# One fused kernel on one core: the order of the first batch's plan, with w3 times w_out moved to its front

## The chip, the core and the metric

The kernel runs on one core of one Trainium2 chip. The core has TensorE (PE, matrix products into PSUM banks), VectorE (DVE), ScalarE (ACT), GpSimd (POOL) and SyncE (SP). ACT, POOL and above all SP issue DMA transfers, which 16 DMA engines carry out. Each engine executes its instructions in order and waits on semaphores for the others. The metric is the device time of one execution in microseconds; lower is better.

## The reference

```python
scores  = scale * x @ state^T;  a  = softmax(scores)      # 8 batches, 8 heads, 512 tokens, 32 state rows, D = 64
xread   = a @ state
scores2 = scale * state @ x^T;  a2 = softmax(scores2)
sread   = a2 @ x
x       = concat([xread, sread], rows), heads side by side   # 4608 x 512
# first FFN: w1, w2 512 x 1024, w3 1024 x 1024, w_out 1024 x 512
a = x @ w1;  b = x @ w2;  h = (a * b) @ w3;  x = h @ w_out
# second FFN: w_gate, w_val 512 x 1536, w_out2 1536 x 512
out = (sigmoid(x @ w_gate) * (x @ w_val)) @ w_out2
```

The weights come as 64-bit floats and are turned into 32-bit ones on the chip. x and state are float32.

## The kernel before

The work is rearranged so that much of it is done once. Since nothing nonlinear stands between w3 and w_out, their product **wp** (1024 x 512) is made once, and y = u wp with u = a * b. The attention's read of the state, times w1 or w2, is the softmax weights times a small product of state and w1 or w2 per batch: a **set** (`StateWeights`, tiles sw), four sets of 256 columns for a batch. The a and b products of a batch are therefore softmax weights (aT) times sets.

Nearly all large products run in split form: each operand is kept as a high and a low part (hi by a ScalarE copy that rounds, lo by a VectorE subtraction), and hi hi + hi lo + lo hi is summed in PSUM, three matmuls in place of one (`products`). A plain float32 product of the same size shows up as two matmul instructions, each of which takes longer.

**The stages.** `plan_start` does the first batch's attention and its a, b and u, and makes wp. Then `ffn1` runs for each batch t: with `slots`, a table of small pieces of other work hung in front of its steps 0 to 11. Steps 0 to 7 (JF = 8) are the a and b products with u = a * b, and steps 8 to 11 (KM = 4) the y products. For t = 0 the steps 0 to 7 are left out, as `plan_start` did them; its y products carry, in their slots, the next batch's sets and attention: at step 8 the end of the plan (`after_wp`), the turned state read (`sreadt`), sets 0 and 1 and the fetches for sets 2 and 3; x turned ahead of steps 8 and 9, scores and the first part of the softmax and sets 2 and 3 at step 10, the rest of the softmax and the split of aT at step 11. Behind all batches follows the second FFN in a stage of its own.

**The plan.** `plan_start` doesn't issue instructions in program order. It lists steps with an engine, an estimated cost and dependences (`plan.add`), and `Plan.order` works out an order from them: PE's and SP's steps keep the order of the list, those of ACT, DVE and POOL are taken greedily, the one with the longest path behind it first. The instructions are then issued in that order by hand. The list before:

1. x and state of batch 0 are loaded, 18 filler transposes on PE (`keep_clock`), x is turned (`xt`), state is turned, scores, both softmaxes (`scores`, `soft1` to `soft3`, `scores2`, `scores3`), 50 fillers.
2. Quarters of w1 and w2 (`quarter(q)`: four loads of 0.52 MB each, converted by `convert` to float32, stored for later batches to w12_d), then `make(q)`, the set, kept in plain float32 (tag swp); 24 fillers ahead of the first products; `pab(j)`: the a and b products for two j per set, plain, with ACT copying a to asb and DVE multiplying it by b to uw. The exponentials of the second softmax are turned (`a2t`) and the state read (`sread`) in between.
3. w_out in eight tiles (`wo_load`, `wo_split`: high part wo, low part wol), w3 in sixteen half rows (`w3_load`, and `w3_turn`: four transposes on PE, then high and low part w3t). `wp_sum(f, ks)` adds 24 matmuls for four k into one PSUM bank, for each of the eight rows f of wp in two halves; `wp_out` writes wp's high and low parts.
4. The u of all j are split into high and low parts (`u_split`), next batch's x is loaded (`load_x`, eight transfers), and quarters 0 and 1 of w1 and w2 are fetched back from w12_d for batch 1 (`nxt.fetch`).

A conversion is two ACT passes (lines 196 and 197) and three DVE passes (198, 202, 206). Raw 64-bit tiles have seven homes (`raw_tile`: three in pool cv, two in pw, two in the buffers that later hold aT); `Ring` tells a step which earlier step must free its buffer. Turned w3 tiles have three buffers and the set's and w3's PSUM tiles two banks.

Of the kernel before, what the change touches and what calls it, by code (L numbers as in the profile page):

```python
# [17 lines left out]
DRAM = bass.MemoryType.DRAM  # L18

# [98 lines left out]
def tile_state_attention__then__gated_ffns(  # L118
# [144 lines left out]
    with tc.manual_schedule(engines={mybir.EngineType.PE}):  # L263
# [15 lines left out]
        def attention(b, plain=False):  # L279
# [4 lines left out]
            def xt(g):  # L284
                def turn():
                    if g == 0:
# [186 lines left out]
            return before, after  # L473
# [16 lines left out]
        def state_turn(h4):  # L490
            pt = z["p", h4] = ps_main.tile([P, 512], F32, tag="m", name="pt")
# [72 lines left out]
        u0 = []  # L564

        def plan_start(cur, nxt):
# [4 lines left out]
            raws, rs, ms, wqs = Ring(7), Ring(2), Ring(3), Ring(2)  # L571
            ats, mains, ys_, asbs, w3s = Ring(2), Ring(4), Ring(2), Ring(2), Ring(3)
            cell = {}

# [5 lines left out]
            def raw_tile(n):  # L580
                if n % 7 < 3:
                    return cv.tile([P, 512, 2], U32, name="raw", bufs=3)
                if n % 7 < 5:
                    return pw.tile([P, 512, 2], U32, name="raw", bufs=2)
                return at.tile([P, 512, 2], U32, tag=f"aT{n % 7 - 5}", name="raw")

            def convert(src, place, *deps):
                n = len(raws.users)
                raw_free, raw_users = raws.take()
# [3 lines left out]
                def load():  # L593
                    c["raw"] = raw_tile(n)
# [8 lines left out]
                got = add("sp", 0.48, load, raw_free, load=LOAD)  # L603
# [12 lines left out]
            def load_half(i):  # L616
# [8 lines left out]
            xs = [add("sp", 0.48, lambda i=i: load_half(i), load=1.7) for i in range(2)]  # L625

            zs = [
                add("sp" if j < 2 else "act", 0.45, lambda j=j: load_z(0, j, (nc.sync, nc.scalar)[j // 2]), load=0.4)
                for j in range(4)
            ]  # L630

# [5 lines left out]
            placed = []  # L637
            for g in range(G):
                placed.append(add("act", 0.52, lambda g=g: place_x(g), xs[g // 2], *placed[-1:]))

            wq_users = []

            def quarter(q):
                free, users = wqs.take()
                wq_users.append(users)
# [8 lines left out]
                for i in range(4):  # L654
                    a, h = divmod(i, 2)
                    src = (w1, w2)[a][2 * h * P : 2 * (h + 1) * P, 2 * q * WQ : 2 * (q + 1) * WQ]
                    d, _ = convert(src.rearrange("(k p) f -> p k f", p=P), lambda i=i: place(i), free, *out[:1])
# [12 lines left out]
            def keep_clock(n):  # L670
                def go():
                    if "clock" not in cell:
                        cell["clock"] = ps_main.tile([P, 512], F32, tag="m", name="clock")
# [5 lines left out]
            clock_free, clock_users = mains.take()  # L679
            keep_clock(18)  # L680
            turned = []
            for g in range(G):
                free, users = ats.take()
                parts = xt(g)
                p = chain(parts[:1], free, placed[g])
                turned.append(chain(parts[1:], p))
                users.append(turned[-1])
            free, users = mains.take()
            p = add("pe", 0.44, lambda: state_turn(0), zs, free)
            st_out = add("act", 0.49, lambda: state_out(0), p)  # L690
            users.append(st_out)
            free = [ats.take() for _ in range(2)]
            parts = scores()
            p = chain(parts[:1], [f for f, _ in free], turned, st_out)
            d = chain(parts[1:], p)
            soft = chain(soft1() + soft2() + soft3(), d)
            e2 = [chain(scores2(k), p) for k in range(2)]
            for k in range(2):
                free[k][1].extend([d, e2[k]])
            r2 = chain(scores3(), e2)  # L700
            keep_clock(50)

            quarters = [quarter(0)]
            sets = {}

            def make(q):
# [5 lines left out]

                def out(k):
                    if k == 0:
                        cur.done[q] = [pb.tile([P, 2, 2, WQ], F32, tag="sw0", name="swp", bufs=4)]
                    copy("act", cur.done[q][0][:, k].rearrange("p a f -> p (a f)"), cell["ps", q][k])

                p = add("pe", 1.0, product, [f for f, _ in free], quarters[q], st_out)
                wq_users[q].append(p)
                o = []  # L720
                for k in range(2):
                    o.append(add("act", 0.49, lambda k=k: out(k), p, *o))
                    free[k][1].append(o[-1])
                sets[q] = o

            uw = {}

            def pab(j):
                ps = []
                for a in range(2):  # L730
# [7 lines left out]
                    ps.append((add("pe", 1.76, product, free, sets[j // 2], soft), users))  # L738
# [6 lines left out]
                def mult():  # L745
                    asb = cell["asb", j]
                    cell["uw", j] = (
                        pu.tile([P, 512], F32, tag="u", name="uw", bufs=2 * JF) if j < JF - 1 else asb
                    )
                    nc.vector.tensor_tensor(  # L750
                        out=cell["uw", j], in0=asb, in1=cell["pab", j, 1], op=ALU.mult
                    )
# [5 lines left out]
                users.append(o1)  # L758
                uw[j] = o1
# [19 lines left out]
            zs1 = []  # L779
            make(0)  # L780
            keep_clock(24)
            quarters.append(quarter(1))
            pab(0)
            pab(1)
            make(1)
            for k in range(2):
                free, users = ats.take()
                parts = a2t(k)
                p = chain(parts[:1], free, e2[k], soft, *([cell["a2", 0]] if k else []))
                cell["a2", k] = chain(parts[1:], p)  # L790
                users.append(cell["a2", k])
            quarters.append(quarter(2))
            pab(2)
            pab(3)
            make(2)
            free, users = ats.take()
            parts = sread()
            p = chain(parts[:1], free, cell["a2", 0], cell["a2", 1])
            users.append(chain(parts[1:], p, r2))
            quarters.append(quarter(3))  # L800
            zs1 = [
                add("sp", 0.45, lambda j=j: load_z(1, j, nc.sync), st_out, load=0.4) for j in range(4)
            ]
            pab(4)
            pab(5)
            make(3)
            free, users = mains.take()
            p = add("pe", 0.44, lambda: state_turn(1), zs1, free)
            users.append(add("act", 0.49, lambda: state_out(1), p))
            for k in range(HALF):  # L810
                wo_load(k)
            w3_load(0)
            pab(6)
            pab(7)

            wo = {}

            def wo_tile(k, i):
                if "wo" not in cell:
                    cell["wo"] = pw.tile([P, JF, DM], F32R, name="wo0", bufs=1)  # L820
                    cell["wol"] = [
                        pb.tile([P, 2, DM], F32R, tag="sw1", name="wol", bufs=4) for _ in range(JF // 2)
                    ]
                return cell["wol"][k // 2][:, k % 2] if i else cell["wo"][:, k]
# [43 lines left out]
            def wp_sum(f, ks):  # L868
                start = ks[0] == 0
                if start:  # L870
                    wp_users[f] = mains.take()
                js = sorted({2 * f + k // 4 for k in ks})

                def product():
                    if start:
                        cell["wp", f] = ps_main.tile([P, 512], F32, tag="m", name="pwp")
                    pairs = [
                        (
                            [t[:, k % 4] for t in cell["w3t", 2 * f + k // 4]],
                            (wo_tile(k, 0), wo_tile(k, 1)),  # L880
                        )
                        for k in ks
                    ]
                    products((cell["wp", f], pairs), begin=start, end=ks[-1] == JF - 1)

                p = add(
                    "pe", len(ks) * 0.69, product, wp_users[f][0] if start else None,
                    [wo[k] for k in ks], [w3t[j][0] for j in js],
                )
                for j in js:  # L890
                    w3t[j][1].append(p)
                return p
# [6 lines left out]
            turns = list(range(0, JF, 2)) + list(range(1, JF, 2)) + list(range(JF, 2 * JF))  # L899
            todo_w3 = turns[1:]  # L900

            def w3_next():
                if todo_w3:
                    w3_load(todo_w3.pop(0))

            for k in range(HALF):
                wo_split(k)
            w3_turn(0)
            for f in range(HALF):
                w3_next()  # L910
                wo_load(HALF + f)
                w3_turn(turns[f + 1])
                wp_sum(f, range(HALF))
                wo_split(HALF + f)
            w3_next()
            w3_next()
            for f in range(JF):
                for i in (2 * f + 3,) if f + 1 < HALF else (2 * f + 1, 2 * f + 2):
                    if i < 2 * JF and i not in w3t:
                        w3_turn(i)  # L920
# [744 lines left out]
```

## Time and profile before

| what | value |
|---|---|
| median of 3 runs | 1299.44 us (1298.42 to 1300.76) |
| profiled execution: time, span | 1299.36 us, 1296.9 us |
| PE busy | 1273.8 us, 98% of the span, 7816 matmuls |
| VectorE, ScalarE busy | 951.6 us (73%), 668.8 us (52%) |
| plan's last PE product ends | 113.80 us from the span's start |
| batch 1's a and b products run steadily from | 144.48 us |

The span runs from the first to the last instruction; the execution's time is a little more. Busy time on PE overlaps between neighbouring matmuls, so the time of a group is read from the start of its first instruction to the start of what follows.

### The profile page before, as it was taken

The page shows a single profiled execution, that of the slowest core. Times are in us where ns is not written, and L with a number is a line of the kernel's source. Part 1 is how long each engine was busy: PE and PEld are TensorE (multiplying, and loading weights), DVE is VectorE, ACT ScalarE, POOL GpSimd, SP SyncE. Part 2 cuts the span into 40 slices and gives each one's busy share as a digit, 9 for nine tenths or more (in the row PEclk, how much of TensorE's full clock was granted, in tenths as well). Part 3 has the DMA queues.
Part 4 walks back from the last instruction along what each step waited for, and adds up shares of the span by engine and source line. Part 5 has one row for each costly group of instructions (what it writes and reads, how often), then busy time and mean ns, then how long its engine had stood idle before and what let it go on. Part 6 is the DMA issues. An engine that isn't in the chain of part 4 may idle for free.

```text
span 1296.9 us, 21521 instructions
## 1 busy us (share of the span) xinstructions
PE 1273.8 (98%) x7816; PEld 1100.1 (85%) x7816; DVE 951.6 (73%) x1839; ACT 668.8 (52%) x1307; POOL 86.7 (7%) x162
## 2 busy tenths in 40 slices
PE   8999999999999999999999999999999999999997
PEld 5487778878787788988887888889999999999996
DVE  6893888797897966165869666688686867687666
ACT  6993667677576655233525333363344444434432
POOL 0000000000000000000000410003100210012000
PEclk9999999999999999999999999999999999999999
DMA  9984496978878732496766868667888889878853
GB/s 308 357 275 140 171 302 241 327 258 299 306 244 291 280 152 88 130 316 193 255 197 176 251 207 244 193 193 253 286 291 261 260 277 296 260 250 280 258 185 98
DMA packets 169120, 312.85 MB, mean 241 GB/s; under 512 B 45368, under 2 KB 63288, under 8 KB 162104
## 3 DMA queue, kind: packets, MB, share of 16 engines
q1 hardware_dynamic: 152948, 257.08, 62.1%
q0 software_dynamic: 9344, 44.57, 9.4%
q10 hardware_dynamic: 6724, 9.83, 2.2%
q8 instruction: 62, 1.02, 0.3%
q14 instruction: 42, 0.34, 0.1%
HBM read 256.38 MB, written 55.05 MB: 240 GB/s over the span
## 4 chain that ended last, share of the span: by engine, by line
PE 86%; DVE 8%; ACT 3%; DMA 1%; issue 1%; ACTq 0%; SPq 0%; DVEq 0%
PE psA L1392 20%; PE po L1562 16%; PE psB L1392 10%; PE pab L225 9%; PE py L225 9%; PE pab L228 5%; PE psC L1392 4%; PE py L228 4%; PE pwp L225 2%; PE psw L533 2%; DVE y L1123 1%; PE pwp L228 1%; PE pxt L290 1%; DVE p L1428 1%; DVE ph L1123 1%; DMA wq<-w12d 1%
## 5 line engine op out<-in xcount | busy, mean ns | idle before, releaser
L1392 PE MATMUL psA<-y,wt 128*128 128x384 f32 (+1 forms) x1440 | 299.8, 356 | 0.0
L1392 PEld LDWEIGHTS psA<-y,wt 128*128 128x128 f32 x1440 | 258.9, 188 | 22.6
L1562 PE MATMUL po<-ph,wo 128*128 128x384 f32 (+1 forms) x1260 | 251.6, 357 | 5.4 <-ACT sv L158 2.8
L1562 PEld LDWEIGHTS po<-ph,wo 128*128 128x128 f32 x1260 | 225.1, 188 | 29.3 <-ACT sv L158 6.0
L158 ACT ACTIVATE u<-psA 128x384 f32<-128x384 f32 (+1 forms) x120 | 64.0, 533 | 228.2 <-PE psA L1392 213.4
L1392 PE MATMUL psB<-y,wt 128*128 128x384 f32 (+1 forms) x720 | 159.5, 356 | 0.0
L1392 PEld LDWEIGHTS psB<-y,wt 128*128 128x128 f32 x720 | 130.0, 188 | 11.2
L225 PE MATMUL py<-u,wp 128*128 128x512 f32 (+1 forms) x576 | 131.8, 381 | 0.0
L225 PEld LDWEIGHTS py<-u,wp 128*128 128x128 f32 x576 | 102.8, 188 | 27.2 <-issue 7.9
L225 PE MATMUL pab<-aT,sw 128*128 128x512 f32 x448 | 122.1, 394 | 0.8 <-DVE aT L163 0.8
L1514 DVE TENSOR_TENSOR acc<-po,acc 128x384 f32<-128x384 f32 (+1 forms) x140 | 83.0, 607 | 31.2 <-PE po L1562 30.8
L1486 POOL DMA_DIRECT2D out<-sv x112 | 61.6, 550 | 599.9 <-DVE sv L1481 593.5
L225 PEld LDWEIGHTS pab<-aT,sw 128*128 128x128 f32 x448 | 82.6, 188 | 17.7 <-DVE aT L163 1.1
L1419 DVE TENSOR_TENSOR p<-psB,u 128x384 f32<-128x384 f32 (+1 forms) x60 | 36.6, 610 | 81.8 <-ACT u L158 74.2
L1421 ACT ACTIVATE p<-p 128x384 f32<-128x384 f32 (+1 forms) x90 | 50.7, 563 | 82.5 <-DVE p L1419 82.5
L1392 PE MATMUL psC<-y,wt 128*128 128x384 f32 (+1 forms) x360 | 79.8, 356 | 0.0
L1123 DVE TENSOR_TENSOR ph<-p,ph 128x384 fp32r<-128x384 f32 (+1 forms) x120 | 70.3, 607 | 7.4 <-ACT ph L158 6.4
L1392 PEld LDWEIGHTS psC<-y,wt 128*128 128x128 f32 x360 | 65.0, 188 | 5.6
L228 PE MATMUL pab<-aT,sw 128*128 128x512 f32 x224 | 69.1, 390 | 0.0
L228 PE MATMUL py<-u,wp 128*128 128x512 f32 (+1 forms) x288 | 67.7, 377 | 0.0
L158 ACT ACTIVATE ph<-p 128x384 fp32r<-128x384 f32 (+1 forms) x120 | 63.5, 564 | 0.2 <-DVE p L1123 0.2
L158 ACT ACTIVATE ph<-t 128x384 fp32r<-128x384 f32 (+1 forms) x90 | 49.4, 564 | 26.6 <-DVE t L1123 26.4
(146 smaller groups left out, 1857.5 us busy)
## 6 DMA issues: line engine op xcount, KB each, us to landing
wt<-wd SPq DMA_DIRECT2D x420, 256.0 KB, 3.5
wo<-wod SPq DMA_DIRECT2D x105, 512.0 KB, 3.7
wq<-w12d SPq DMA_DIRECT2D x32, 1024.0 KB, 8.1
raw<-in_moe_w SPq DMA_DIRECT2D x32, 512.0 KB, 6.5
wd<-wstb POOLq DMA_DIRECT2D x12, 1024.0 KB, 5.4
raw<-in_moe_w_out SPq DMA_DIRECT2D x20, 512.0 KB, 5.8
wd<-wsta POOLq DMA_DIRECT2D x12, 768.0 KB, 4.1
xn<-in_x SPq DMA_DIRECT2D x56, 128.0 KB, 6.6
```

What stands on the lines that cost most here:

```text
L158: return nc.scalar.activation(out=o, in_=i, func=AF.Copy)
L225: nc.tensor.matmul(o, w[i], xx[k], start=begin and n == 0 and i + k == 0, stop=False)
L228: nc.tensor.matmul(o, w[1 - late], xx[late], start=False, stop=end and n == len(pairs) - 1)
L290: nc.tensor.transpose(pt[:, c * P : (c + 1) * P], xn[b][:, g, c].rearrange("p a d -> p (a d)"), ident,)
L533: nc.tensor.matmul(pts[k][NS * g : NS * g + NS, a * WQ : (a + 1) * WQ], stT[64 * k : 64 * k + 64, g, self.b * NS : (self.b + 1) * NS], w[6 ...
L1123: nc.vector.tensor_tensor(out=o, in0=x0, in1=x1, op=ALU.subtract)
L1392: nc.tensor.matmul(o, w[:, i, kb * P : (kb + 1) * P], xx[kb][h], start=start, stop=i == 1 and kb == 1, skip_group_check=True,)
L1419: nc.vector.tensor_tensor(out=t, in0=o, in1=kept[a, what], op=ALU.add)
L1421: later(2, 0.0, lambda: nc.scalar.activation(out=t, in_=t, func=AF.Sigmoid))
L1486: nc.gpsimd.dma_start(out=dst[:, :, i * P : (i + 1) * P], in_=t[32 * i : 32 * i + 32].rearrange("t j d e -> t j (d e)"),)
L1514: nc.vector.tensor_tensor(out=acc[d, cc], in0=o, in1=acc[d, cc], op=ALU.add)
L1562: nc.tensor.matmul(o, w[:, jj, i, d * P : (d + 1) * P], x[h], start=k in (1, 6, 2) and jj == 0 and i + h == 0, stop=jj == 1 and i == 1, sk ...
```

## The change

The steps of the plan are now listed by a string of tokens, and their order is another:

- `o` n fillers; `w` and `s` load and split a w_out tile; `l` and `t` load and turn a w3 half row; `d` n: a quarter sum of wp, row n / 4, quarter n % 4 (two k, six matmuls). `x`, `g`: load and turn batch 0's x; `z`, `i`: load and turn state; `h`: scores and softmaxes; `v`: split of batch 0's aT; `e`, `r`: turned exponentials, state read; `q`, `m`, `p`: quarter of w1 and w2, set, a and b products; `y`, `k`: load and turn batch 1's x.
- So w_out and w3 are loaded first and their product stands ahead of the attention's scores and of the a and b products, which come last. The order of the quarters within a row of wp is free.
- The sets of batch 0 are split (8 low parts more on VectorE), aT of batch 0 is split, and the a and b products run in split form. u is split behind each product, without uw.
- The fillers number 60, 38 and 14 in place of 18, 50 and 24, in a bank of another pool.
- The low parts of w_out lie in the ring of the u tiles (sixteen buffers) and no longer in the sets' buffers. Once `v` has split aT, raw tiles have five homes.
- Batch 1's x is turned in the plan. Its scores and first softmax go out at y step 9 in place of 10, the rest at 10; sets 0 and 1 and the fetches of quarters 2 and 3 come ahead of y step 9 in place of 8, sets 2 and 3 ahead of 11 in place of 10.

```diff
+SEQUENCE = """
+o60 w3 l4 t4 o38 w4 s3 w2 s4 s2 l0 t0 o14 w1 w0 d1 l2 d9 x0 s0 w6 s1 t2
+d8 d0 l6 g0 t6 s6 d5 w5 l3 s5 d4 l1 t3 d12 l5 g1 w7 t1 l7 d6 l8 s7 x1 l9
+d13 l11 t5 q0 d7 d2 t7 d11 t9 d3 t8 l15 z0 d14 d10 d15 d19 d17 l10 i0
+l13 t11 d18 g3 z1 g2 l12 m0 h v d16 t15 d22 t10 d23 t13 d30 l14 d20 d26
+d31 q1 t12 t14 d21 d27 d24 d25 e0 d28 e1 i1 d29 r y m1 p1 k1 k3 p0 q2 p2
+k2 m2 q3 k0 p3 p4 m3 p5 p7 p6
+"""
...
+                if "seven" in turn_:
+                    return (n - turn_["seven"]) % 5
+                return n % 7
...
+                def out_low(k):
+                    minus(flat(1, k), cell["ps", q][k], flat(0, k))
...
+                    lows.append(add("dve", 0.6, lambda k=k: out_low(k), o[-1]))
+                    free[k][1].extend([o[-1], lows[-1]])
+                sets[q] = o + lows
...
-                    ps.append((add("pe", 1.76, product, free, sets[j // 2], soft), users))
+                    ps.append((add("pe", 1.39, product, free, sets[j // 2], cell["soft"]), users))
...
+                    nc.vector.tensor_tensor(out=asb, in0=asb, in1=cell["pab", j, 1], op=ALU.mult)
...
+                h = add("act", 0.52, high, o1, *cell.get("us", []))
+                l = add("dve", 0.6, lambda: minus(t[1], cell["asb", j], t[0]), h)
...
-            def wp_sum(f, ks):
-                start = ks[0] == 0
+            def wp_sum(f, quarter):
+                ks = range(2 * quarter, 2 * quarter + 2)
+                start = f not in wp_users
...
+            def halves():
+                homes_ = homes.get(5), homes.get(6)
+                turn_["seven"] = turn_["n"]
 
                 def high():
+                    tr = cell["tr"] = aT[b][0]
+                    aT[b] = [at.tile([P, 2, S], F32R, name=f"aT{i}") for i in range(2)]
+                    copy("act", aT[b][0], tr)
+
+                h = add("act", 0.97, high, cell["plain"], homes_)
+                l = add("dve", 1.12, lambda: minus(aT[b][1], cell["tr"], aT[b][0]), h)
+                return h, l
...
+            def next_load():
+                cell["y"] = add("sp", 6.7, lambda: load_x(order[1]), placed, load=3.0)
+
+            def next_turn(g):
+                free, users = ats.take()
+                parts = next_xt(g)
+                p = chain(parts[:1], free, cell["y"], cell["read"], cell["soft"])
+                users.append(chain(parts[1:], p))
...
+            for token in SEQUENCE.split():
+                do(token)
...
                 if t == 0:
-                    slots[JF].append(lambda nxt=nxt: nxt.make(0, 1))
-                    slots[JF].append(lambda get=get: get(2, 3))
+                    slots[JF + 1].append(lambda nxt=nxt: nxt.make(0, 1))
+                    slots[JF + 1].append(lambda get=get: get(2, 3))
                     for i, fns in before.items():
-                        slots[i + 2] += fns
-                    slots[JF + 2].insert(1, lambda nxt=nxt: nxt.make(2, 3))
+                        if i >= JF:
+                            slots[i + 1] += fns
+                    slots[JF + 3].append(lambda nxt=nxt: nxt.make(2, 3))
```

## Rows read from the trace of the kernel before

**Rows 1.** The page, part 1: busy time, share of the span, instructions.
```profile
PE 1273.8 (98%) x7816; PEld 1100.1 (85%) x7816; DVE 951.6 (73%) x1839; ACT 668.8 (52%) x1307; POOL 86.7 (7%) x162
```

**Rows 2.** Busy time by stage: stretch, length, engines, granted clock, DMA share, GB/s.
```profile
0.00:26.30 26.30, 20.17 (x160) 16.37 (x161) 15.53 (x30) 17.42 (x29) 1.45 (x8) 0.94 0.91 309
26.30:113.80 87.50, 85.51 (x494) 57.79 (x493) 74.26 (x153) 70.48 (x127) 2.19 (x3) 1.00 0.86 280
...
144.48:1296.90 1152.42, 1138.30 (x6906) 1003.49 (x6906) 845.49 (x1631) 567.98 (x1129) 83.03 (x151) 1.00 0.74 239
9.21:104.54 95.33, 90.14 (x577) 61.12 (x576) 88.49 (x180) 81.75 (x146) 2.88 (x4) 0.98 0.96 318
10.00:40.00 30.00, 27.08 (x189) 16.87 (x190) 25.06 (x52) 22.21 (x40) 1.25 (x2) 0.94 0.98 326
...
50.00:60.00 10.00, 8.92 (x53) 3.78 (x52) 9.67 (x21) 9.94 (x19) 0.00 (x0) 1.00 1.01 410
```

**Rows 3.** PE's timeline, first 35 us: start, length, what, idle before.
```profile
1.37 4.00 PE L675 MATMUL clock<-ident 128*128 128x128 f32 x18 [1.37 <-POOL ident masks.py:199]
...
11.48 5.68 PE L675 MATMUL clock<-ident 128*128 128x128 f32 x50
...
20.82 1.24 PE L533 MATMUL psw<-wq,stT 64*32 64x256 f32 x16 [2.44 <-DVE wq L206]
21.99 4.51 PE L675 MATMUL clock<-ident 128*128 128x128 f32 x24
26.33 7.03 PE L219 MATMUL pab<-a2tr,swp 128*128 128x512 f32 x16
33.30 1.09 PE L533 MATMUL psw<-wq,stT 64*32 64x256 f32 x32
```

**Rows 4.** PE's timeline: last sum of wp, then batch 1's a and b.
```profile
107.83 0.60 PE L845 MATMUL pw<-ident,m 128*128 128x128 f32 x4
108.19 0.48 PE L225 MATMUL pwp<-wo,w3t 128*128 128x512 f32 x1
...
113.80 0.27 PE L450 MATMUL psrt<-ident,sr 128*128 128x128 f32 x1
...
144.48 0.98 PE L225 MATMUL pab<-aT,sw 128*128 128x512 f32 x3 [0.76 <-DVE aT L163]
...
145.76 1.08 PE L225 MATMUL pab<-aT,sw 128*128 128x512 f32 x4
...
147.15 1.07 PE L225 MATMUL pab<-aT,sw 128*128 128x512 f32 x4
```

**Rows 5.** Timeline of SP's queue and of ScalarE at the start.
```profile
0.74 1.00 SPq L620 DMA_DIRECT2D xz<-in_x  x2
...
2.82 30.52 SPq L171 DMA_DIRECT2D raw<-in_moe_w  x16
...
4.97 1.15 ACT L158 ACTIVATE xn<-xz 128x512 f32<-128x512 f32 x2 [1.87 <-DMA xz<-in_x]
```

**Rows 6.** VectorE's timeline, three neighbours near 99 us.
```profile
98.76 0.70 DVE L206 CUSTOM_DVE_ANT_0 m<-m,r 128x1024 uint16<-128x1024 uint16 x1
99.36 0.49 DVE L198 TENSOR_SCALAR r<-raw 128x512 uint16<-128x512 uint16 x1
99.70 0.44 DVE L202 TENSOR_SCALAR m<-m 128x512 uint32<-128x512 uint32 x1
```

**Rows 7.** DMA issues, first 150 us: KB each, median us from issue to landing.
```profile
raw<-in_moe_w SPq DMA_DIRECT2D x32, 512.0 KB, 6.5
wq<-w12d SPq DMA_DIRECT2D x6, 1024.0 KB, 6.2
w12d<-wq POOLq DMA_DIRECT2D x4, 1024.0 KB, 7.9
```

**Rows 8.** As rows 2, two stretches of the start.
```profile
5.00:11.00 6.00, 3.70 (x39) 2.37 (x37) 0.48 (x2) 5.54 (x11) 0.00 (x0) 1.00 1.09 339
...
23.00:24.00 1.00, 1.00 (x6) 1.00 (x5) 1.00 (x2) 1.00 (x3) 0.00 (x0) 0.50 1.00 406
```

More of the change, by code (lines that the diff above doesn't have):

```diff
@@ L285, in turn @@
                 def turn():
-                    if g == 0:
+                    if "xT" not in t:
                         t["xT"] = at.tile([P, G, S], F32, tag="xT", name="xT")
@@ L601, in first @@
                     c["parts"][0]()
-                got = add("sp", 0.48, load, raw_free, load=LOAD)
+                got = add("sp", issue, load, raw_free, load=LOAD)
                 a0 = add("act", 0.55, first, got, r_free, *deps)
@@ L656, in quarter @@
                     src = (w1, w2)[a][2 * h * P : 2 * (h + 1) * P, 2 * q * WQ : 2 * (q + 1) * WQ]
-                    d, _ = convert(src.rearrange("(k p) f -> p k f", p=P), lambda i=i: place(i), free, *out[:1])
+                    d, _ = convert(src.rearrange("(k p) f -> p k f", p=P), lambda i=i: place(i), free, *out[:1], issue=0.82)
                     out.append(d)
@@ L677, in keep_clock @@
                 clock_users.append(add("pe", n * 0.11, go, clock_free))
[L679 to L703, printed above, removed]
+            clock_free, clock_users = ats.take()
             sets = {}
@@ L778, in plan_start @@
             HALF = JF // 2
[L779 to L814, printed above, removed]
             wo = {}
@@ L820, in wo_tile @@
                     cell["wo"] = pw.tile([P, JF, DM], F32R, name="wo0", bufs=1)
[L821 to L824, printed above, removed]
+                if i and ("wol", k) not in cell:
+                    cell["wol", k] = pu.tile([P, DM], F32R, tag="u", name="wol", bufs=2 * JF)
+                return cell["wol", k] if i else cell["wo"][:, k]
             def minus(o, x0, x1):
@@ L866, in plan_start @@
             wp_users = {}
-            def wp_sum(f, ks):
-                start = ks[0] == 0
+            def wp_sum(f, quarter):
+                ks = range(2 * quarter, 2 * quarter + 2)
+                start = f not in wp_users
                 if start:
-                    wp_users[f] = mains.take()
-                js = sorted({2 * f + k // 4 for k in ks})
+                    wp_users[f] = (*mains.take(), [])
+                wp_users[f][2].append(quarter)
+                end = len(wp_users[f][2]) == JF // 2
+                j = 2 * f + quarter // 2
                 def product():
@@ L897, in wp_out @@
                 wp_users[f][1].extend([a, d])
[L899 to L914, printed above, removed]
@@ L936, in plan_start, with x_load, state_load @@
-            for j in range(JF):
-                u_split(j)
-            add("sp", 6.7, lambda: load_x(order[1]), placed, load=3.0)
+            xs = []
+            zs = {}
+            placed = []
+            turned = []
+            def x_load(i):
+                xs.append(add("sp", 0.48, lambda: load_half(i), load=1.7))
+                for g in range(2 * i, 2 * i + 2):
+                    placed.append(add("act", 0.52, lambda g=g: place_x(g), xs[i], *placed[-1:]))
+            def state_load(h4, *deps):
+                zs[h4] = [
+                    add("sp", 0.45, lambda j=j: load_z(h4, j, nc.sync), *deps, load=0.4) for j in range(4)
+                ]
@@ new lines, in x_turn, with state_in @@
+            def x_turn(g):
+                free, users = ats.take()
+                parts = xt(g)
+                p = chain(parts[:1], free, placed[g])
+                turned.append(chain(parts[1:], p))
+                users.append(turned[-1])
+            def state_in(h4):
+                free, users = ats.take()
+                p = add("pe", 0.44, lambda: state_turn(h4), zs[h4], free)
+                cell["st", h4] = add("act", 0.49, lambda: state_out(h4), p)
+                users.append(cell["st", h4])
@@ new lines, in attend @@
+            def attend():
+                free = [ats.take() for _ in range(2)]
+                parts = scores()
+                p = chain(parts[:1], [f for f, _ in free], turned, cell["st", 0])
+                d = chain(parts[1:], p)
+                soft = chain(soft1() + soft2() + soft3(), d)
+                cell["plain"] = soft
+                cell["e2"] = [chain(scores2(k), p) for k in range(2)]
+                for k in range(2):
+                    free[k][1].extend([d, cell["e2"][k]])
+                cell["r2"] = chain(scores3(), cell["e2"])
@@ new lines, in exp_turn, with state_read @@
+            def exp_turn(k):
+                free, users = ats.take()
+                parts = a2t(k)
+                p = chain(parts[:1], free, cell["e2"][k], cell["plain"], *([cell["a2", 0]] if k else []))
+                cell["a2", k] = chain(parts[1:], p)
+                users.append(cell["a2", k])
+            def state_read():
+                free, users = ats.take()
+                parts = sread()
+                p = cell["read"] = chain(parts[:1], free, cell["a2", 0], cell["a2", 1])
+                users.append(chain(parts[1:], p, cell["r2"]))
@@ L953, in tile_state_attention__then__gated_ffns @@
         nxt = StateWeights(order[1])
+        before1, after1, next_xt = attention(order[1])
         sreadt = plan_start(cur, nxt)
@@ L1161, in tile_state_attention__then__gated_ffns @@
                     slots[0].append((lambda go=go: behind(go)) if t < 2 else go)
-                before, after = attention(order[t + 1])
+                before, after = attention(order[t + 1])[:2] if t else (before1, after1)
                 def get(*qs, nxt=nxt):
```

153 lines of the change are left out of this document (89 added, 64 removed).

## The prediction, made before the change was run

> **What bounds the kernel now.** I read the page first: TensorE (PE) is busy for 98% of the span [rows 1]. An average hides a slow start, so the busy time by stage came next [rows 2]. From 144.48 us to the end PE is busy 1138.3 of 1152.4 us: that part follows PE, and if the work ahead of it ends earlier, the whole run does. Two stages lie ahead: up to 113.8 us the first batch's plan, which ends with w3 times w_out, and up to 144.48 us the y products, behind which batch 1's a and b products run steadily.
>
> PE's timeline of the plan [rows 3] shows what the first 26.3 us hold: 18, 50 and 24 filler transposes that compute nothing, and short steps of the attention. The first dense work (a and b products of batch 0) starts at 26.33, because it needs x, the softmax and a weight quarter. From then to 113.80 PE is busy 85.5 of 87.5 us [rows 2]. So three things can shorten the time before 144.48: dense work that starts earlier, less work on PE, and the stall just ahead of 144.48, where PE waits for the split of batch 1's attention, aT [rows 4].
>
> VectorE is close behind: from its first operation at 9.21 us to 104.54 us it is busy 88.5 of 95.3 us (7.2% idle), and 25.1 of 30 us between 10 and 40 us; ScalarE has 81.8 in the same 95.3 [rows 2]. So a shorter PE chain may be held up by VectorE.
>
> **The change, part by part.** I work out E, the time at which the plan's last PE product ends (113.80 us before), and then the y stage.
>
> *Front.* PE's order is fixed: 60 fillers, a turn of w3, 38 fillers, a turn, 14 fillers, the first quarter sum. A filler took 4.00/18 = 0.222 us at first and 5.68/50 = 0.114 us later [rows 3]. With 18 at the first pace: 1.37 + 4.00 + 42 x 0.114 = 10.2 us; then a turn of 0.36 (107.83 to 108.19 [rows 4]), 38 x 0.114, 0.36 and 14 x 0.114 put the first sum at 16.8. Its operands need five loads of 0.52 MB. The first transfer issued at 0.74 is used at 4.97 [rows 5], and the stretch moves 309 GB/s [rows 2], 1.7 us a load, so the fifth lands at 11.8. Conversion (some 1.9), turn, copy and low part (1.5) make 15.2. The fillers cover that by 1.6 us, and their own length is what counts.
>
> *PE's work from there.* 32 quarter sums of 6 matmuls: a full sum of 24 took 113.80 - 108.19 = 5.61 [rows 4], so 1.40 each: 44.8. 14 turns at 0.36: 5.0. The 16 a and b products, now in split parts: 145.76 to 147.15 is 1.39 a product [rows 4]: 22.2. The plain ones took 33.30 - 26.33 = 6.97 for four, 27.9 for all [rows 3], so 5.7 us of work go. Four sets at 1.09 [rows 3]: 4.4. Eight x turns, four of them the next batch's, of four transposes each like a w3 turn: 2.9. Two state turns and two of the exponentials, the same, and scores and state read at the price of a set: 3.6. Sum 82.9, so E = 99.7 without a gap.
>
> *VectorE.* Its pitch is 0.60 us for the last step of a conversion and for any product or low part of 512, 0.34 for each of the two short steps [rows 6]; a conversion is 1.27. 40 conversions (50.8), 56 operations of 0.60 (33.6; the sets' 8 low parts are new), the softmax (7.8: five operations over 1024 at 1.1, ten smaller) and aT's new low part (1.1, about two of 512) make 93.3 us; 87.4 before. It can start at 5.0. Two places decide. For the sum d7 it must have done 8 w_out tiles and 6 w3 tiles (1.27 + 0.60 each) and a seventh conversion: 27.5 us, so 32.5. PE reaches d7 at 16.8 + 9 x 1.40 + 5 x 0.36 + 2 x 0.36 = 31.9. They meet, so VectorE's losses become PE's gap: 7.2% idle is 2.1 us, a gap of 2.7. The other place is the last set, m3: all but 7.2 us of VectorE's work lies ahead of its operands, so they are there at 5.0 + 86.1 = 91.1 plus losses, and 9.6 us of PE follow (0.2, 1.09 and six products). At 7.2% over all of it (6.7 us) E is 107.4, a gap of 7.7. I take 5, near the middle, as the row of 10 to 40 us idles more than the average and the later part less. E = 104.7. ScalarE gains only 3 us of work and stays behind VectorE.
>
> *The queues.* SP issues the same 40 weight loads, x, state, next x and fetches; two state loads come to it from ScalarE's queue, and x moves behind eight weight loads. Next x's 8 issues now stand ahead of the last two quarters' 8 loads, which are needed some 20 us later: nothing. Raw buffers fall from 7 to 5 once aT is split: 6.5 us to land [rows 7] and some 2.5 of conversion, over 5, is 1.8 us a load; 13 loads are left, 23 us, and PE has over 40 us of work to cover them (from the scores on): nothing. The fetch of w1 and w2's quarter 1 for batch 1 waits for the store of quarter 3: about 1 + 7.9 us behind its conversion, then 0.5 + 6.2 to land [rows 7], 15.6 in all; PE reads it at E + 5.8, at least 15.4 behind. Bounds 0 and 2 us; I take 0, as the set will seldom be the exact limit. Behind it on PE would stand the scores and three y products.
>
> *The y stage* was 144.48 - 113.80 = 30.68 us. The next batch's four x turns leave it (1.4, counted above), and as its scores go out one y product earlier (24 matmuls, 5.6 us), aT is in time: the wait of 0.76 goes [rows 4]. 28.5 stay, so steady products start at E + 28.5 = 133.2, not 144.48: 11.3 us less. The profiled execution took 1299.36 us (its span 1296.9; the median of the runs is 1299.44), so **1288 us**. In general the time is 1183.4 + E.
>
> **The clock.** From 23 to 24 us PE's granted clock was 0.50, its lower level of 1.2 GHz [rows 8], behind an idle gap of 2.44 us; PE ran only filler transposes from 21.99 to 26.33 [rows 3], and from 26.3 on the clock is 1.00 [rows 2]. From 5 to 11 us PE was busy only 3.7 of 6 us and the clock stayed at 1.00 [rows 8].
> The Trainium skill ("TensorE: Matmul & The Clock Gate", Part 4: PE-mode transpose) says that transposes don't bring the full clock, as they don't count as busy in the same way. The rows around 22 to 26 us speak against that. By it the new start's fillers are of no use, and the result is that of the second rival below, 1298 us.
>
> **The rivals.**
> - *Loads set the start.* Before, 16 weight loads went out in 30.52 us, 1.91 each [rows 5]. At that pace the 16th issue, the last that d7 needs, is usable at 0.74 + 15 x 1.91 + 6.5 + 3.0 (conversion and split) = 38.9, against 31.9. A gap of 7 to 11 (with VectorE's) gives 1290 to 1294. For it: the 16 DMA engines are busy 0.91 of the start. Against it: between 50 and 60 us, among w_out and w3 loads, 410 GB/s were moved [rows 2].
> - *The clock falls to 1.2 GHz in the loose stretch up to d7.* Its 15.1 us of PE become 30.2 and d7 starts at 47.0, not 36.9: E = 114.8, 1298 us, no change that can be measured. Against it: [rows 8], and that the stretch is nearly full.
> - *Slower: VectorE runs dry.* Its instructions stay in the planned order, and one late operand holds all behind it. Through m3, E = 100.7 + loss. The change breaks even at E = 116.0, a loss of 15.3 us (15% of its time), and is slower by over 0.2% from 17.9. Between 10 and 40 us it idled 16% [rows 2]; 20% all through (21.5 us) gives 1306. Against it: over 95 us it was 7.2%.
>
> **Numbers.** Forecast (1283 to 1292) 0.64; loads 0.18; clock 0.07; slower 0.04; PE meets no gap and ends under 1283, 0.07. Less than 0.2% (2.6 us) can't be told from no change: the three runs spread by 2.3. Range 1283 to 1296: the first two cases. Faster 0.90, same 0.05, slower 0.05.
>
> **What would show it.** Right: first sum at 16 to 17 us; PE gaps of 3 to 8 us in all, most of them before d7; E near 105; no wait for aT where batch 1 starts. Wrong: a granted clock of 0.5 between 17 and 45 us; VectorE idle over 12 us; PE waiting for the last set, or for the fetched quarter behind the first y product; later stages that lengthen.

## The result and the profile after

| kernel | median of 4 runs | range |
|---|---|---|
| before | 1299.45 us | 1298.42 to 1300.76 |
| changed | 1287.9 us | 1285.18 to 1288.95 |

The ratio is 0.9907, 95% interval 0.9895 to 0.992: 11.55 us less. The forecast was 1288 us. The profiled execution took 1287.98 us, its span 1286.2.

The page, part 1, of the changed kernel answers to [rows 1]:
```profile
PE 1267.1 (99%) x7868; PEld 1107.4 (86%) x7868; DVE 957.4 (74%) x1848; ACT 669.1 (52%) x1308; POOL 86.6 (7%) x162
```
Its busy time by stage, columns as in [rows 2]; the third stretch is the y stage, the fourth begins where batch 1's a and b products run steadily, and the last is the stretch that VectorE's idle share is read from:
```profile
0.00:17.50 17.50, 16.13 (x121) 16.06 (x122) 11.30 (x23) 12.34 (x20) 0.75 (x7) 1.00 0.90 333
17.50:103.90 86.40, 84.91 (x601) 67.33 (x600) 84.00 (x168) 78.03 (x141) 2.70 (x4) 1.00 0.90 285
103.91:132.02 28.11, 27.25 (x243) 20.48 (x241) 17.18 (x27) 10.12 (x18) 0.00 (x0) 1.00 0.66 234
132.02:1286.20 1154.18, 1138.85 (x6908) 1003.55 (x6906) 844.93 (x1631) 568.57 (x1130) 83.12 (x151) 1.00 0.73 239
...
4.00:100.00 96.00, 94.51 (x692) 77.61 (x692) 93.23 (x187) 86.74 (x155) 2.70 (x4) 1.00 0.91 294
```
The dense work begins at 17.3 us instead of 26.3, and from there VectorE is nearly as full as PE. PE's timeline, beside [rows 3] and [rows 4]:
```profile
1.37 9.58 PE L684 MATMUL clock<-ident 128*128 128x128 f32 x60 [1.37 <-POOL ident masks.py:199]
10.79 0.60 PE L805 MATMUL pw<-ident,m 128*128 128x128 f32 x4
11.23 4.31 PE L684 MATMUL clock<-ident 128*128 128x128 f32 x38
15.38 0.65 PE L805 MATMUL pw<-ident,m 128*128 128x128 f32 x4
15.86 1.69 PE L684 MATMUL clock<-ident 128*128 128x128 f32 x14
17.31 0.48 PE L235 MATMUL pwp<-wo,w3t 128*128 128x512 f32 x1
17.63 0.39 PE L235 MATMUL pwp<-wol,w3t 128*128 128x512 f32 x1
17.86 0.40 PE L235 MATMUL pwp<-wo,w3t 128*128 128x512 f32 x1
...
21.23 0.63 PE L805 MATMUL pw<-ident,m 128*128 128x128 f32 x4 [0.91 <-DVE m L216]
...
28.97 0.63 PE L805 MATMUL pw<-ident,m 128*128 128x128 f32 x4 [0.37 <-DVE m L216]
...
103.91 0.27 PE L460 MATMUL psrt<-ident,sr 128*128 128x128 f32 x1
...
111.53 1.10 PE L543 MATMUL psw<-wq,stT 64*32 64x256 f32 x32 [0.85 <-DMA wq<-w12d]
112.42 1.07 PE L323 MATMUL psc<-xT,stT 64*32 64x512 f32 x16
...
132.02 1.07 PE L235 MATMUL pab<-aT,sw 128*128 128x512 f32 x4
```
The first matmul behind the fillers takes 0.32 us (17.31 to 17.63), the next 0.23. Between 17.31 and 103.91 PE waits for data twice, 0.91 and 0.37 us. The first a and b product of batch 1 has no wait where 0.76 stood in [rows 4]; the set at 111.53 has a new one, for a fetched quarter.

Steady products start 12.46 us earlier than the row of 144.48 in [rows 4]. The profiled span fell by only 10.7, because the same work behind them took 1154.18 instead of 1152.42 us. Over the thirteen profiled executions of this study (the two here and eleven of the experiments) that part took 1152.4 to 1155.3 us, and no experiment alters its work. So I read the 1.8 us as scatter between executions and look for causes ahead of it.

### The profile page after: what moved, and what is told of

The parts are those of the page before. It is cut to its first block, busy times and chain, and to the rows that moved or that the text cites. A ratio compares the mean times of both kernels' runs of the same rounds, so it can differ in the third digit from the quotient of the medians.

```text
span 1286.2 us, 21643 instructions
## 1 busy us (share of the span) xinstructions
PE 1267.1 (99%) x7868; PEld 1107.4 (86%) x7868; DVE 957.4 (74%) x1848; ACT 669.1 (52%) x1308; POOL 86.6 (7%) x162
## 4 chain that ended last, share of the span: by engine, by line
PE 81%; DVE 9%; ACT 5%; DMA 3%; issue 1%; SPq 0%; ACTq 0%; POOL 0%; DVEq 0%; POOLq 0%
PE psA L1438 20%; PE po L1608 16%; PE psB L1438 10%; PE pab L235 9%; PE py L235 8%; PE pab L238 5%; PE psC L1438 4%; PE py L238 4%; DMA wq<-w12d 2%; PE psw L543 2%; DVE y L1168 1%; ACT r L207 1%; DVE p L1474 1%; DVE ph L1168 1%; PE pxt L300 1%
## 5 line engine op out<-in xcount | busy, mean ns | idle before, releaser
L235 PE MATMUL pab<-aT,sw 128*128 128x512 f32 x512 | 139.4, 394 | 0.0
L235 PEld LDWEIGHTS py<-u,wp 128*128 128x128 f32 x576 | 102.8, 188 | 28.2 <-issue 8.3
L235 PEld LDWEIGHTS pab<-aT,sw 128*128 128x128 f32 x512 | 94.4, 188 | 19.2 <-DVE s L356 0.4
L238 PE MATMUL pab<-aT,sw 128*128 128x512 f32 x256 | 78.9, 390 | 0.0
```

Of the source, the lines that this page charges most:

```text
L235: nc.tensor.matmul(o, w[i], xx[k], start=begin and n == 0 and i + k == 0, stop=False)
L238: nc.tensor.matmul(o, w[1 - late], xx[late], start=False, stop=end and n == len(pairs) - 1)
```

## The experiments

E is, as in the prediction, the time at which the plan's last product ends: 113.80 before, 103.9 changed. Ratios are to the kernel before, with 95% intervals. The plan orders VectorE's and ScalarE's work greedily by the costs given to it, so in a kernel with altered costs some of their steps also change places.

**What the split is worth.** Sets and aT of batch 0 unsplit, everything else as changed:
```diff
-                            pb.tile([P, 2, 2, WQ], F32R, tag=f"sw{i}", name=f"sw{i}", bufs=4)
-                            for i in range(2)
+                        cur.done[q] = [pb.tile([P, 2, 2, WQ], F32, tag="sw0", name="swp", bufs=4)]
...
-                    ps.append((add("pe", 1.39, product, free, sets[j // 2], cell["soft"]), users))
+                    ps.append((add("pe", 1.76, product, free, sets[j // 2], cell["soft"]), users))
```


> The new order with the sets and aT of batch 0 kept whole, and the a and b products plain, as before the change: no low parts of the sets or of aT (5.9 us less on VectorE), 5.7 us more on PE. Theory (the plan is PE's chain, VectorE has slack behind it): E, where the plan's last product ends, goes from 103.9 to 109 to 110 us, and the run from 1287.9 to about 1293.5. Rival (VectorE's work through the last set ends the plan): E moves by less than 2 us, as VectorE is relieved by as much as PE is loaded, and the run stays under 1290.

1291.25 us, ratio 0.9935 (0.9923 to 0.9948), E 109.0. So the split moves E by 5.1 us and the run by 3.35; the other 8.2 of the 11.55 come from the rest of the change together (order, fillers, y stage). E moved as the theory says, the run a little less: steady products start at 136.06, 4.04 later, because this kernel has no wait for a fetched quarter and its y stage takes 27.0 us. The 0.7 us that are left are within the scatter between executions.

**What the move in the y stage is worth.** Batch 1's x turned in the y stage, sets and scores one y product earlier, as before; the plan's order stays:
```diff
-d31 q1 t12 t14 d21 d27 d24 d25 e0 d28 e1 i1 d29 r y m1 p1 k1 k3 p0 q2 p2
-k2 m2 q3 k0 p3 p4 m3 p5 p7 p6
+d31 q1 t12 t14 d21 d27 d24 d25 e0 d28 e1 i1 d29 r y m1 p1 p0 q2 p2
+m2 q3 p3 p4 m3 p5 p7 p6
...
-                    slots[JF + 1].append(lambda nxt=nxt: nxt.make(0, 1))
+                    slots[JF].append(lambda nxt=nxt: nxt.make(0, 1))
```


> The y stage as before the change: batch 1's x turned there, sets 0 and 1 ahead of the first y product, scores one y product later. Theory (PE then needs the quarter fetched for batch 1 at the plan's end, and that lands some 16.8 us behind the last quarter's conversion): E 102.2, a wait of 6 to 8 us for the fetched quarter ahead of the first y product, a wait of about 0.8 for aT, batch 1 steady 5 to 8 us later than 132.0, run 1293 to 1296. Rival (the y stage's change is worth only the wait for aT): the run stays within 1287 to 1290.

1296.66 us, ratio 0.9975 (0.9966 to 0.9985), E 103.5. PE's timeline of the plan's last set and of the y stage, then the busy time of one stretch of the latter:
```profile
94.64 0.64 PE L543 MATMUL psw<-wq,stT 64*32 64x256 f32 x8 [1.24 <-DVE wq L216]
...
109.80 1.96 PE L543 MATMUL psw<-wq,stT 64*32 64x256 f32 x32 [4.99 <-DMA wq<-w12d]
111.69 1.97 PE L300 MATMUL pxt<-ident,xn 128*128 128x128 f32 x8
113.31 4.00 PE L235 MATMUL py<-u,wp 128*128 128x512 f32 x16
...
118.97 1.03 PE L300 MATMUL pxt<-ident,xn 128*128 128x128 f32 x8
...
140.66 0.96 PE L235 MATMUL pab<-aT,sw 128*128 128x512 f32 x3 [0.76 <-DVE aT L173]
```
```profile
110.00:112.00 2.00, 2.00 (x34) 0.85 (x23) 0.00 (x0) 0.16 (x1) 0.00 (x0) 0.50 0.78 324
```
The stage takes 37.1 us instead of 28.1. Of these 9.0, 4.14 are the longer wait for the fetch (4.99 against 0.85), 0.76 the wait for aT, 2.4 the turns (1.62 and 0.79), 0.9 the set behind the wait (1.96 against 1.10), at a granted clock of 0.50, and 0.5 one matmul that went ahead of the wait for aT; 0.3 stay unassigned.

I had expected an E of 102.2, since batch 1's four turns, 1.7 us in the changed kernel's plan, are gone from it. E fell by 0.4 only: PE waited 1.24 us for VectorE's last conversion instead. So the turns cost the new plan next to nothing, and VectorE sets its end.

The same move alone in the old order (x turned in the plan, the slots as in the change):
```diff
+            for g in range(G):
+                free, users = ats.take()
+                parts = next_xt(g)
+                p = chain(parts[:1], free, y, soft)
+                users.append(chain(parts[1:], p))
```


> The kernel before, with the y stage of the change alone: batch 1's x turned at the plan's end, scores and sets one step later or earlier as in the change. Theory (in the old order the fetch lands long ahead, so the y stage is worth just the wait for aT of 0.76 us): plan's end 115.5, no wait for aT, batch 1 steady at 143.5 to 144, run 1298.5 to 1299.5. Rival (the y stage saves several us by itself): run under 1297.

1298.47 us, ratio 0.999 (0.9981 to 0.9998): 1.3 us (0.3 to 2.5 by the interval), and aT's wait is gone. So the move is worth 8.8 us in the new order and about 1.3 in the old. It is no small extra: the new order ends the plan just behind quarter 3's conversion, and the y product that now stands ahead of the sets covers the round trip of the weights.

**The fillers.** All three groups removed:
```diff
-o60 w3 l4 t4 o38 w4 s3 w2 s4 s2 l0 t0 o14 w1 w0 d1 l2 d9 x0 s0 w6 s1 t2
+w3 l4 t4 w4 s3 w2 s4 s2 l0 t0 w1 w0 d1 l2 d9 x0 s0 w6 s1 t2
```


> No filler transposes in the plan. Theory (the fillers bring PE's clock up and nothing else waits for them, as the first quarter sum waits for its operands until 17.2 us anyway): granted clock 0.50 or a pace of 0.43 us a matmul in the first sums, which start at 17 us; PE loses 2 to 5 us, E 105 to 109. Rival one (transposes don't count for the clock): clock and E as with them, 103 to 104.5. Rival two (the fillers held up the turns): first sum before 16.3 us and E 1 us or more earlier.

1286.04 us, ratio 0.9897 (0.9882 to 0.9912), E 102.8. PE's timeline:
```profile
9.07 1.09 PE L805 MATMUL pw<-ident,m 128*128 128x128 f32 x4 [9.07 <-DVE m L216]
14.24 1.12 PE L805 MATMUL pw<-ident,m 128*128 128x128 f32 x4 [4.08 <-DVE m L216]
16.05 0.80 PE L235 MATMUL pwp<-wo,w3t 128*128 128x512 f32 x1 [0.69 <-ACT w3t L168]
16.64 0.63 PE L235 MATMUL pwp<-wol,w3t 128*128 128x512 f32 x1
17.07 0.63 PE L235 MATMUL pwp<-wo,w3t 128*128 128x512 f32 x1
...
21.73 0.39 PE L235 MATMUL pwp<-wo,w3t 128*128 128x512 f32 x1
21.95 0.39 PE L235 MATMUL pwp<-wol,w3t 128*128 128x512 f32 x1
```
The busy time of one stretch, columns as in [rows 2]:
```profile
16.00:20.00 4.00, 3.95 (x9) 3.14 (x10) 4.00 (x10) 4.00 (x8) 0.00 (x0) 1.00 1.03 410
```
The first sums go at 0.43 us a matmul and later at 0.23: the two levels of the clock, as the fillers gave the higher one from the first sum on. The stretch's granted clock reads 1.00 all the same; the first change of clock that this trace holds comes at 20.2 us, where the pace doubles, so ahead of it only the pace tells the level. In the changed kernel 27 of the 60 fillers start by 7.18 us, 0.21 us apart, and the other 33 by 10.79, 0.11 apart: the pace doubled while nothing but transposes ran. The Trainium skill ("TensorE: Matmul & The Clock Gate", Part 4: PE-mode transpose) says transposes don't bring the full clock; here, with nothing but transposes ahead of it, the first sum ran at 0.23, and without them at 0.43, so the measurement decides against it. But the fillers also stand in PE's queue: the first turn could go at 9.07 and went at 10.79, the second at 14.24 and went at 15.38. VectorE gets the turned row's low part later, and E is 1.1 us later. So the second rival came true, not the theory. PE's two waits are gone without fillers, but its first sums are also slower there; the kernel with fewer fillers tells the two apart.

Two more kernels have the scores ahead of sets 0 and 1 in the y stage, which gives the fetch time. One is without fillers, the other with 42, 34 and 8:
```diff
-                    slots[JF + 1].append(lambda nxt=nxt: nxt.make(0, 1))
-                    slots[JF + 1].append(lambda get=get: get(2, 3))
                     for i, fns in before.items():
                         if i >= JF:
                             slots[i + 1] += fns
+                    slots[JF + 1].append(lambda nxt=nxt: nxt.make(0, 1))
+                    slots[JF + 1].append(lambda get=get: get(2, 3))
```


> No fillers, and scores and softmax of batch 1 ahead of its sets 0 and 1 at the step behind the first y product, so that the fetched quarter has 0.9 us more to land. Theory (E without fillers is 102.8, and the wait for the fetched quarter goes): no wait for it, run 1285 to 1286. Rival (what is won there is lost to a later wait): run as without fillers alone, 1286, or more.

> Fillers cut to 42, 34 and 8, which ends each lot ahead of the operands of the turn or sum behind it; scores ahead of sets 0 and 1 as well. Theory (up to d7 VectorE's conversions set the pace, so a PE at full clock there only waits longer): first sum at 16 us at 0.23 us a matmul, gaps of 1 to 3 us up to d7, E 102 to 103.5 as without fillers. Rival (the 2 us that PE loses at the low clock without fillers are lost for good): E 100.5 to 101.5, run 1284.

Without fillers: 1285.49 us, ratio 0.9893 (0.9878 to 0.9908), E 102.9, no wait for the fetch. With fewer: 1286.03, ratio 0.9895 (0.9882 to 0.9909), E 102.8. PE's waits for conversions up to 150 us of the latter (total, times, longest):
```profile
PE pw L805 <- DVE m L216: 3.9, 5, 1.3
```
Its turns go at 9.10 and 14.37, nearly as early as without fillers, its first sum at 15.73 and at 0.23 us a matmul. Yet E is that of the kernel without fillers: PE only waits longer for conversions, 1.6 of the 3.9 us behind the first sum, where the kernel without fillers waits for none. The slow first matmuls of the kernel without fillers lie in time that VectorE takes anyway, and what the fillers of the change cost is the delay of the turns. The first is the lowest median here, 2.4 us under the change, but the intervals overlap, so I don't call it faster. The wait for the fetch came in one of the two (0.86 us, with fewer fillers) at the same E: the landing varies, and the reordering does not settle it.

**VectorE's margin.** One short step of a conversion done twice (the second writes the same again), fifteen times early, up to d7, or fifteen times late; 5.1 us by [rows 6]:
```diff
-                d0 = add("dve", 0.34, lambda: c["parts"][2](), a0)
+                more = turn_["n"] <= 15
+                d0 = add("dve", 0.68 if more else 0.34, lambda: [c["parts"][2]() for _ in range(1 + more)], a0)
```


> The first short VectorE step of the first 15 conversions is done twice: 15 x 0.34 = 5.1 us more VectorE work, nearly all of it ahead of the sum d7. Theory of the prediction (VectorE and PE meet at d7, what VectorE loses there is PE's gap): PE gaps up to d7 grow by 4 to 5 us, E 107.5 to 109, run 1292. Rival (VectorE runs ahead of PE with work that isn't urgent and can be put off): gaps grow by less than 2 us, E under 106, run under 1290.

> The counterpart of the early load: the first short VectorE step is done twice in the last 15 conversions (w3's last ones and three quarters of w1 and w2), 5.1 us more VectorE work behind d7. Theory (only the stretch up to d7 is tight; behind it PE is ahead of nothing but has VectorE's results in time): E moves by less than 1.5 us from 103.9, PE waits for no conversion behind 60 us beyond 1 us in all, run under 1290. Rival (the second bound of the prediction, VectorE's whole work through the last set, is as tight): E moves by 4 to 6 us and PE waits for the last set.

Early: 1295.05 us, ratio 0.9964 (0.9952 to 0.9977), E 112.0. Late: 1294.15, ratio 0.9955 (0.9941 to 0.9969), E 112.7. Early, PE's timeline and two stretches of busy time:
```profile
23.55 1.08 PE L806 MATMUL pw<-ident,m 128*128 128x128 f32 x4 [2.63 <-DVE m L216]
24.29 0.78 PE L235 MATMUL pwp<-wo,w3t 128*128 128x512 f32 x1
24.86 0.63 PE L235 MATMUL pwp<-wol,w3t 128*128 128x512 f32 x1
25.29 0.63 PE L235 MATMUL pwp<-wo,w3t 128*128 128x512 f32 x1
```
```profile
17.50:112.00 94.50, 88.26 (x604) 70.14 (x603) 89.40 (x179) 80.12 (x142) 3.37 (x4) 0.96 0.83 263
24.00:26.00 2.00, 2.00 (x7) 1.71 (x7) 1.93 (x7) 1.63 (x4) 0.00 (x0) 0.50 0.67 252
```
Of the 8.1 us, 4.75 are PE's idle time (94.50 - 88.26 = 6.24 against 1.49) and 3.35 its longer busy time: behind each of two long waits the granted clock is 0.50 for a stretch, with the 0.43 us a matmul seen without fillers. Late, the busy time, then PE's timeline of the last set:
```profile
17.50:112.70 95.20, 89.42 (x600) 68.21 (x599) 90.54 (x183) 79.11 (x141) 2.70 (x4) 0.98 0.86 274
```
```profile
98.24 1.41 PE L543 MATMUL psw<-wq,stT 64*32 64x256 f32 x16
101.71 1.66 PE L543 MATMUL psw<-wq,stT 64*32 64x256 f32 x16 [2.06 <-DVE wq L216]
```
Of the 8.8 us, 4.3 are idle time (95.20 - 89.42 = 5.78 against 1.49) and 4.5 longer busy time, of which the granted clock, 0.98 over the stretch, can account for 1.9 at most. The last set, whose operands now come half by half, lasts from 98.24 to 103.29; in the changed kernel it took 1.0 us (94.59 to 95.61).

I had expected slack behind d7; there is less than 1 us of it. The prediction's second place, the last sets, binds as well: 5.1 us on VectorE cost 8 to 9 us of E at either place.

**Relieving VectorE.** In the kernel without fillers and with the scores first, six of the eight low parts of w_out go to GpSimd; in a second kernel four low parts of u as well:
```diff
+                if k not in (2, 3):
+                    wo[k] = a, add("pool", 1.3, lambda: nc.gpsimd.tensor_tensor(
+                        out=wo_tile(k, 1), in0=cell["wof", k], in1=wo_tile(k, 0).bitcast(F32), op=ALU.subtract
+                    ), a)
+                    return
```


> As the run without fillers and with scores first, and six of w_out's eight low parts are subtracted by GpSimd in place of VectorE: 3.6 us less on VectorE, all ahead of d7. Theory (VectorE sets the pace of the whole plan, so what it is relieved of comes back one for one or nearly): E from 102.9 to 99.5 to 101, run from 1285.5 to 1282 to 1284. Rival (GpSimd's subtraction takes so long, or slows VectorE's own steps beside it, that the quarter sums wait for it): E 102.5 or more, VectorE's steps longer than 0.60 us beside it.

> As the run before, and the low parts of u of the first four j go to GpSimd as well: 2.4 us less on VectorE behind 75 us. Theory (the second bound, through the last set, is as tight): E 0.5 to 2 us under that of the run with six low parts. Rival (by then PE is the bound): E within 0.4 us of it.

1289.72 us, ratio 0.993 (0.9917 to 0.9943), E 108.0; with u 1292.31, 0.9948 (0.9936 to 0.9961), E 109.6. Both are slower than their base. VectorE's and GpSimd's timelines of the first kernel:
```profile
13.23 1.48 DVE L216 CUSTOM_DVE_ANT_0 m<-m,r 128x1024 uint16<-128x1024 uint16 x1 [0.20 <-ACT r L207]
```
```profile
12.61 1.54 POOL L792 TENSOR_TENSOR wol<-wof,wo 128x512 fp32r<-128x512 f32 x1 [11.29 <-ACT wo L168]
```
This conversion's last step, which reads two SBUF operands, begins during a GpSimd subtraction and takes 1.48 us, where it takes 0.70 alone [rows 6]. It ends 0.56 us behind the subtraction (14.71 against 14.15), as if it had begun when that ended. Five of the six subtractions hold up a last step so (1.30 to 1.77 us). Beside the sixth, the last step at 30.29 had begun before it and took 0.68; the first step behind that, with one operand, took 1.55 instead of 0.46. The Trainium skill ("SBUF — State Buffer", SBUF: two separate sides) says the two engines share a port pair as an exclusive lock, held for the whole instruction; the trace agrees in that these steps waited for its end. Not every step did: a second step (one operand, uint32) at 37.60 kept its 0.41 beside the subtraction of 37.47, and a product with one operand in PSUM its 0.69, as VectorE's and GpSimd's timelines of the second kernel show:
```profile
102.46 0.69 DVE L740 TENSOR_TENSOR asb<-asb,pab 128x512 f32<-128x512 f32 x1 [1.21 <-ACT asb L168]
```
```profile
102.34 1.31 POOL L756 TENSOR_TENSOR u<-asb,u 128x512 fp32r<-128x512 f32 x1
```
In the first kernel, up to 50 us, conversions' last steps took a mean of 936 ns (11 of w3) and 848 (8 of w_out) instead of 683 and 688, and 21 first steps 510 instead of 463: 2.8 + 1.3 + 1.0 = 5.1 us lost for six steps of 0.60 taken off, 1.5 us in all. VectorE also idles longer: it is busy 41.42 of the 45 us from 5 to 50, against 43.95 in the base. That makes 4.0 of the 5.1 us by which E moved; the rest is not traced. PE itself waited for a GpSimd result once, 0.9 us.

**Which loads go first.** x loaded ahead of the weights:
```diff
-o60 w3 l4 t4 o38 w4 s3 w2 s4 s2 l0 t0 o14 w1 w0 d1 l2 d9 x0 s0 w6 s1 t2
+o60 x0 x1 w3 l4 t4 o38 w4 s3 w2 s4 s2 l0 t0 o14 w1 w0 d1 l2 d9 s0 w6 s1 t2
```


> The changed kernel with x loaded ahead of the weights, as before the change: 1.05 MB, 2.6 to 3.3 us at 320 to 400 GB/s, ahead of the first w_out tile. Theory (VectorE is the bound from its first load on): first sum 2 to 3 us later than 17.3, E 106 to 107.5, run 1290.5. Rival (the start is covered by fillers and slack): E within 1 us of 103.9, run under 1289.5.

1289.01 us, ratio 0.9918 (0.9903 to 0.9933). The first sum starts 2.84 us later (20.15), E is 106.8, 2.9 later: the plan keeps its length and slides with the first sum. Not all of the 2.84 is the load: PE waits 1.97 us for the first turn, from 12 to 16 us the granted clock is 0.57, and the 38 fillers take 5.4 us (12.84 to 18.27) instead of 4.15. The run does not separate the two. Of the 2.9 us of E, 1.9 are left at 133.90, where steady products start, since the wait for the fetch is gone.

## Why the prediction was right, point by point

- **Front**: first sum at 17.31, forecast 16.8. The 60 fillers took 0.6 us more, as 27 of them, not 18, went at the first pace. That their own length counts held: without them the sum starts at 16.05, 1.26 earlier, where I had 1.6. What I left out is that they also hold back the turns and with them VectorE: they cost E 1.1.
- **PE's work from there**: 86.6 us to E, less 1.3 of waits, is 85.3, forecast 82.9. The step that was mis-sized took a sum of 24 and a turn from rows that run in a row. In the new order kinds alternate: the first matmul behind a turn takes 0.32 instead of 0.23, so that a quarter sum takes 1.47 there, against 1.38 in a row, and a turn of x 0.44, not 0.36. Sums (46.3 us against 44.8) and turns of x (3.7 against 2.9) make up 2.3 of the 2.4.
- **VectorE's gap**: 1.3 us, forecast 5 and bounds 2.7 to 7.7. It was the idle share that was off: VectorE is busy 93.23 of 96.0 us, 2.9% idle, not the 7.2% of the old order; it also began at 4.0 us, not 5.0. The places were right: both waits lie ahead of d7, 5.1 us more on VectorE gave gaps there at once, and 5.1 us more behind d7 a wait for the last set.
- **E** is 103.9 against 104.7 since these two errors, 2.4 too little and 3.7 too much, nearly cancel; the front adds 0.5. They are not independent: where VectorE sets the pace, PE's work takes the place of waiting, as the plan without batch 1's turns showed (1.7 us less work, E 0.4 lower). That the run hit 1288 to 0.1 us is luck: E came 0.8 lower and the y stage 0.4 lower, the part behind them took 1.8 longer, and the execution's excess over its span was 0.7 less.
- **Queues**: the quarter was usable 16.75 us behind its conversion, forecast 15.6 at best and bounds of 0 and 2 for the wait; 0.85 came where I took 0. The fetch was issued at 105.47, 10.4 us behind the store's issue at 95.07, where I had 7.9. PE came to the set 6.8 us behind E, not 5.8, as the set of quarter 0 stands ahead of it; else the wait would have been longer. The margin was thin enough for the landing's variation to decide: over the five kernels that waited for this quarter, it was usable 15.2 to 17.7 us behind its conversion.
- **The signs**: no wait for aT and E near 105 came. The first sum (17.31, not 16 to 17) and the gaps (1.3, not 3 to 8) missed, and one sign of being wrong came true, the wait for the fetched quarter.
- **The y stage**: 28.11, forecast 28.5; aT's wait went. I priced the move at 0.76 and two small terms; its real worth, 8.8 us, was hidden in the sum, since I checked the fetch only against the new slots.
- **Rivals**: loads did not set the start; 1.3 us of waits, not 7 to 11. The clock stayed at 1.00. VectorE running dry did not come, but its price is steeper than I said: behind waits of 2.1 to 2.9 us the lower clock came on top, and 5.1 us cost 8.1 and 8.8. If that slope holds, break-even lies nearer than a loss of 15.3; no run went that far.

Left open: what varies the landing of the fetch, and the 1.8 us behind 132 us beyond its being within the scatter.

## What to carry to other kernels

Where a late stage follows one engine, bring its dense work forward to the first point at which its operands exist, and then ask the new order what became just too late: here the y stage's order was worth 8.8 us, and about 1.3 in the old order. Count a chain's instructions in the neighbourhood in which they will stand, and take an engine's idle share from a stretch as full as the new one. A filler ahead of a turn that another engine waits for can cost more than the clock it buys.

## What the hardware showed that I had not expected

- A stream of nothing but 128x128 transposes brought the higher clock: their pace went from 0.21 to 0.11 us at 7.2 us, and the first sum ran at 0.23 us a matmul. Without it the first matmuls took 0.43 us.
- At waits of 2.1, 2.6, 2.9 and 5.0 us in the dense work, and of 2.0 us among the fillers, the granted clock fell to 0.50; at waits of up to 1.3 us in these kernels it stayed at 1.00.
- A VectorE step with two SBUF operands that began during a GpSimd subtraction of 1.3 to 1.7 us took 1.3 to 1.8 us instead of 0.69. A product with one operand in PSUM kept its 0.69 us.
